# Reordering the first loads, casting and plain loads in a chain, and normalising two PSUM banks at once in a pooled-attention + MLP kernel

## Chip, cores, metric

One core of a Trainium2 chip. The metric is the time of one execution in device microseconds. All runs compared below are of the fast state; a ratio is the mean time of one kernel's fast runs over the mean of the other's fast runs of the same rounds, so it is not quite the ratio of the medians that are quoted.

## The reference

Attention whose keys and values are averaged over groups of 8 positions, followed by an MLP on every token.

```python
# q, k, v: (8, 8, 576, 64) float32: batch, head, position, dimension
k_p = k.reshape(B, H, 72, 8, D).mean(axis=3)      # 72 pooled keys per head
v_p = v.reshape(B, H, 72, 8, D).mean(axis=3)
attn = softmax(q @ k_p.T / sqrt(D))
x = (attn @ v_p).transpose(0, 2, 1, 3).reshape(4608, 512)
h = x @ w_in                                       # (512, 2048)
out = (h - tanh(h)) @ w_out                        # (2048, 512)
```

## The kernel before

In the lines of the profile PE is TensorE, the matrix engine, DVE is VectorE, ACT is ScalarE, POOL is GpSimd, and SP only issues transfers. PSUM, which PE writes to, is used as eight banks (the changed kernel's tile `PS` is 128 x 8 x 512 in fp32). A casting load turns fp32 into bf16 on the way (the page lists 512 KB for a quarter of w1, which is 1 MB in fp32); w1 and w2 come as four such loads each, w2(0) being the first quarter of w2. Filler (`warm_pe`) is matmuls whose result nobody uses.

Tokens are worked in nine groups of 512 (one batch is 576 tokens). A group has a hidden phase (16 tiles of 4 matmuls with w1, each followed by tanh and a subtraction) and an o phase (64 matmuls with w2). Attention of the next batch is woven into the o phase of the present group. Group 0 can't start until batch 0's attention has gone through by itself. Keys come as 8 heads x 72 pooled rows: 128 rows of each pair of heads go into "pairs" 0 to 3, and the 16 rows left over of each of the four pairs share a fifth tile ("leftover"), with index `NM` = 4.

```python
    load_main(k_pairs, k_raw[0], 0, 0, 1)               # SP: pair 0
    load_q0(0, 2)                                       # ScalarE's queue: heads 0, 1
    load_main(k_pairs, k_raw[0], 0, 1, 2)               # SP: pair 1
    load_q0(2, 4)
    load_main(k_pairs, k_raw[0], 0, 2, 4)               # SP: pairs 2, 3 (512 KB)
    load_q0(4, 8)                                       # heads 4 to 7 (512 KB)
    load_dense(k_pairs, k_raw[0], 0, nc.scalar)         # leftover keys (128 KB)
    load_dense(v_pairs, v_raw[1], 0, nc.scalar)         # leftover V (128 KB)
    ...
    nc.gpsimd.memset(q_bf[64:128, R, :, :], 0.0)
    ...                                                 # masks
    nc.gpsimd.dma_start(out=v_bf[:, 0:NM, :], in_=v_pairs[0, 0:128, :, :])   # V, cast to bf16
    ...
    for c in range(4):
        load_w1(c)                                      # casting loads, GpSimd's queue
    load_w2(0)
    load_w2(1)
    ...
    after(load_k(1), w1_dmas[1])                        # batch 1's keys wait for w1's 2nd quarter
    load_q(1, False)
    load_main(v_pairs, v_raw[1], 1, 0, NM)              # v1, behind q on SP
    ...
    pool_k(0, nc.vector, 2, 4)
    warm_pe(6)                                          # filler matmuls
    k_turn(2, 4)
    pool_k(0, nc.vector, NM, NT)
    ...
    av_half(0, 0, 0, xs[0], ps_all)                     # eight of these: AV of one half block,
    ...                                                 # 1 reciprocal, 1 product each
```

The softmax here doesn't subtract the row's maximum and nothing guards it: scores larger than these inputs give would overflow.

## Time and profile before

| | before |
|---|---|
| time, median of 3 | 300.87 us (300.75 to 301.25) |
| span, TensorE clock | 299.1 us, 1.000 |
| PE starts batch 0's AV (attention times V) | 14.61 us |
| five half hidden tiles done, PE dense | 21.27 us |
| o phase of group 0 starts | 34.55 us |
| group 1 starts | 54.98 us |
| from group 1's start to the end | 244.1 us |

The last five rows are read from the timeline of PE, by the first matmul of each kind. The prediction shows the other lines of this profile. One more view: the DMA issues of the first 5 us. Its columns are the number of transfers, KB of each, and microseconds from issue to landing.

```profile
k_raw<-in_k_dram SPq DMA_DIRECT2D x1, 512.0 KB, 6.1
q_raw<-in_q_dram ACTq DMA_DIRECT2D x1, 512.0 KB, 7.1
v_raw<-in_v_dram POOLq DMA_DIRECT2D x1, 512.0 KB, 8.6
k_raw<-in_k_dram ACTq DMA_DIRECT2D x1, 128.0 KB, 7.3
```

Pairs 2, 3 land at 7.83; the second half of q at 8.96, the leftover keys at 9.66. VectorE pools them in that order.

### The profile page before, as it was taken

How to read it: one execution, taken by the hardware profiler on the slowest of the kernel's cores; microseconds unless marked ns; L12 is line 12 of the kernel's file. 1: busy time of each engine (PE TensorE's matmuls, PEld its weight loads, DVE VectorE, ACT ScalarE, POOL GpSimd, SP SyncE). 2: the span in 40 equal slices, each digit the busy share in tenths (PEclk: the TensorE clock that was granted, in tenths of full speed). 3: DMA queues.
4: the chain of work that ended last, by engine and by line, in shares of the span. 5: the costliest groups of instructions: out<-in, count | busy, mean ns of one | idle time of the engine just before them, and what ended most of it. 6: DMA issues, size and time to landing. Idle time of an engine off the chain costs nothing.

```text
span 299.1 us, 4694 instructions
## 1 busy us (share of the span) xinstructions
PE 291.5 (97%) x1671; PEld 142.5 (48%) x1671; DVE 159.1 (53%) x343; ACT 149.4 (50%) x283; POOL 115.5 (39%) x110
## 2 busy tenths in 40 slices
PE   7989999999999999999999999999999999999994
PEld 3454455544544454445444554455445544444443
DVE  5658665673547444753476247716680758108600
ACT  4647583666146633654265516650665166126511
POOL 8500904871496109922971089307940000000000
PEclk9999999999999999999999999999999999999999
DMA  7999999849854998699648974897431430111032
GB/s 251 226 211 278 311 227 310 263 87 328 234 113 99 271 297 134 117 302 245 107 88 235 300 167 94 242 294 159 97 66 35 95 92 0 37 70 36 0 72 70
DMA packets 66183, 49.79 MB, mean 166 GB/s; under 512 B 39920, under 2 KB 52976, under 8 KB 66160
## 3 DMA queue, kind: packets, MB, share of 16 engines
q1 hardware_dynamic: 58832, 42.94, 56.0%
q0 software_dynamic: 4752, 4.72, 9.4%
q10 hardware_dynamic: 2576, 1.84, 2.3%
q8 instruction: 13, 0.21, 0.3%
q14 instruction: 10, 0.08, 0.1%
HBM read 36.70 MB, written 9.44 MB: 154 GB/s over the span
## 4 chain that ended last, share of the span: by engine, by line
PE 85%; DMA 9%; POOL 4%; issue 0%; SPq 0%; ACT 0%; DVE 0%; POOLq 0%
PE o_ps L456 40%; PE hT_ps L428 37%; DMA w1b<-in_moe_w_in_dram 4%; PE x_ps L346 4%; DMA k_raw<-in_k_dram 4%; PE s_ps L298 3%; POOL k_raw L198 1%; DMA out_dram<-o_sb 1%; POOL k_raw L203 1%; POOL kd L206 1%; POOL w2b L510 0%; PE xT_ps L390 0%; POOL v_raw L576 0%; PE qT_ps L171 0%; POOL w1b L503 0%
## 5 line engine op out<-in xcount | busy, mean ns | idle before, releaser
L456 PE MATMUL o_ps<-w2b,gT 128*128 128x512 bf16 x560 | 134.4, 380 | 0.0
L441 DVE TENSOR_TENSOR gT<-hT_ps,t_sb 128x512 bf16<-128x512 f32 x144 | 98.9, 691 | 57.7 <-ACT t_sb L439 57.6
L428 PE MATMUL hT_ps<-xT,w1b 128*128 128x512 bf16 x576 | 126.9, 379 | 0.3 <-ACT xT L397 0.3
L439 ACT ACTIVATE t_sb<-hT_ps 128x512 f32<-128x512 f32 x144 | 85.6, 597 | 38.3 <-PE hT_ps L428 37.5
L428 PEld LDWEIGHTS <-w1b 128*128 128x128 bf16 x576 | 55.9, 98 | 66.5 <-issue 0.4
L456 PEld LDWEIGHTS <-gT 128*128 128x128 bf16 x560 | 52.5, 98 | 52.0 <-issue 1.4
L465 ACT COPY o_sb<-o_ps 128x512 f32<-128x512 f32 x33 | 19.3, 585 | 75.2 <-PE o_ps L456 75.2
L359 DVE RECIPROCAL rden<-x_ps 128x4 f32<-128x4 f32 x80 | 14.2, 177 | 52.5 <-PE x_ps L346 52.0
L360 DVE TENSOR_TENSOR x_sb<-x_ps,rden 128x256 bf16<-128x256 f32 x80 | 34.0, 425 | 3.5 <-DMA xT<-x_sb 0.6
L148 POOL CAST q_bf<-q_raw 128x2048 bf16<-128x2048 f32 x6 | 11.3, 1888 | 59.9 <-issue 34.8
L198 POOL TENSOR_TENSOR k_raw<-k_raw 128x1280 f32<-128x1280 f32 x7 | 20.2, 2886 | 27.4 <-DMA k_raw<-in_k_dram 16.6
L317 ACT ACTIVATE E<-s_ps 128x288 bf16<-128x288 f32 x60 | 21.4, 410 | 13.2 <-PE s_ps L298 13.0
L346 PE MATMUL x_ps<-VB,E 128*128 128x130 bf16 x240 | 20.8, 221 | 0.4 <-ACT xT L397 0.3
L346 PEld LDWEIGHTS <-E 128*128 128x128 bf16 x240 | 16.9, 98 | 8.8 <-DVE VB L230 0.6
L216 POOL TENSOR_TENSOR v_raw<-v_raw 128x1280 f32<-128x1280 f32 x6 | 17.4, 2898 | 0.0
L298 PE MATMUL s_ps<-qT,KB 128*128 128x288 bf16 (+5 forms) x128 | 17.0, 290 | 0.2
L298 PEld LDWEIGHTS <-KB 128*128 128x128 bf16 (+1 forms) x128 | 7.0, 96 | 10.2 <-issue 3.5
L527 PE MATMUL warm_ps<-xT 128*128 128x512 bf16 x29 | 10.2, 465 | 1.3 <-DVE xT L539 1.3
L206 POOL TENSOR_TENSOR kd<-k_raw 128x640 bf16<-128x640 f32 x7 | 10.8, 1540 | 0.5
L203 POOL TENSOR_TENSOR k_raw<-k_raw 128x640 f32<-128x640 f32 x7 | 10.8, 1541 | 0.5
L397 ACT CAST xT<-xT_ps 128x256 bf16<-128x256 f32 (+1 forms) x14 | 5.8, 436 | 8.5 <-PE xT_ps L390 5.1
L219 POOL TENSOR_TENSOR v_raw<-v_raw 128x640 f32<-128x640 f32 x6 | 9.3, 1544 | 0.5
(73 smaller groups left out, 100.7 us busy)
## 6 DMA issues: line engine op xcount, KB each, us to landing
k_raw<-in_k_dram SPq DMA_DIRECT2D x7, 1024.0 KB, 5.9
q_raw<-in_q_dram SPq DMA_DIRECT2D x7, 1024.0 KB, 10.2
v_raw<-in_v_dram SPq DMA_DIRECT2D x7, 1024.0 KB, 9.3
out_dram<-o_sb SPq DMA_DIRECT2D x38, 128.0 KB, 2.4
out_dram<-o_sb SPq DMA_DIRECT2D x16, 256.0 KB, 3.7
w1b<-in_moe_w_in_dram POOLq DMA_DIRECT2D x4, 512.0 KB, 14.2
w2b<-in_moe_w_out_dram POOLq DMA_DIRECT2D x4, 512.0 KB, 16.9
k_raw<-in_k_dram SPq DMA_DIRECT2D x7, 128.0 KB, 5.8
```

Source lines behind the costliest of these rows:

```text
L198: first = eng.tensor_tensor(out=r[:, :, 0:4, :], in0=r[:, :, 0:4, :], in1=r[:, :, 4:8, :], op=ALU.add)
L216: eng.tensor_tensor(out=r[:, :, 0:4, :], in0=r[:, :, 0:4, :], in1=r[:, :, 4:8, :], op=ALU.add)
L298: nc.tensor.matmul(dst[p : p + w], lhsT=KB[b % 2][:, o : o + w], rhs=qTs[b][:, m, c0:c1], start=True, stop=True,)
L317: nc.scalar.activation(out=E[:, t, half * hs : (half + 1) * hs], in_=ps[:, :], func=ACT.Exp, scale=SCALE)
L346: nc.tensor.matmul(ps[:, 2 * n : 2 * n + 2, :].rearrange("p h d -> p (h d)") if n < 2 else ps.rearrange("p (a s) d -> p a s d", s=2)[:, :, ...
L359: nc.vector.reciprocal(out=rden[:, :, :], in_=ps[:, :, D:D1])
L360: nc.vector.tensor_tensor(out=x_sb[:, half, :, :], in0=ps[:, :, 0:D], in1=rden[:, :, :].to_broadcast([128, 4, D]), op=ALU.mult,)
L428: nc.tensor.matmul(h_tiles[i][:, :], lhsT=w1b[:, fb, i * 128 : (i + 1) * 128], rhs=xT[:, fb, tok0 : tok0 + TG], start=(fb == 0), stop=(fb ...
L439: nc.scalar.activation(out=t_sb[:, :], in_=h_ps[:, :], func=ACT.Tanh)
L441: nc.vector.tensor_sub(out=gT[:, :], in0=h_ps[:, :], in1=t_sb[:, :])
L456: nc.tensor.matmul(o_ps[:, :], lhsT=gts[i][:, tb * 128 : (tb + 1) * 128], rhs=w2b[:, i, :], start=(i == 0), stop=(i == NHID - 1),)
L465: (nc.vector.tensor_copy if g == 0 and tb % 2 else nc.scalar.copy)(out=o_sb[:, :], in_=o_ps[:, :])
```

## The change

The intent: (1) leftover keys go ahead of pairs 2, 3 on SP, so that the small tile is out of the way early; (2) PSUM becomes one tile with hand-chosen banks, and the AV of two blocks in two adjoining banks is normalised by one reciprocal and one product; (3) casting loads (w1, w2) and plain loads (batch 1's k, q, v) no longer run side by side but in a chain; (4) batch 1's q comes as nine consecutive rows per partition, without a tail in 256-byte pieces; (5) the last store falls on the last lane of the final waits.

```diff
+    nc.vector.memset(k_raw[0][:, NM, :], 0.0)
     nc.vector.memset(zeros, 0.0)
-    nc.vector.memset(k_raw[0][:, NM, :], 0.0)
...
+    load_dense(k_pairs, k_raw[0], 0)
+    load_q_main(0, 4, 8, nc.scalar)
     load_main(k_pairs, k_raw[0], 0, 2, 4)
-    load_q0(4, 8)
-    load_dense(k_pairs, k_raw[0], 0, nc.scalar)
     load_dense(v_pairs, v_raw[1], 0, nc.scalar)
...
-    nc.gpsimd.memset(q_bf[64:128, R, :, :], 0.0)
...
     nc.gpsimd.dma_start(out=v_bf[:, 0:NM, :], in_=v_pairs[0, 0:128, :, :])
+    nc.gpsimd.memset(q_bf[64:128, R, :, :], 0.0)
...
-    load_w2(0)
-    load_w2(1)
-    after(load_k(1), w1_dmas[1])
-    load_q(1, False)
-    load_main(v_pairs, v_raw[1], 1, 0, NM)
+    qt0 = load_q_tail(0)
+    k1 = load_k(1)
+    load_dense(v_pairs, v_raw[1], 1)
+    load_q_nine(1, 0, nc.sync)
+    load_q_nine(1, 1, nc.sync)
+    after([qt0], w1_dmas[1])
+    load_w2(0)
+    after(w2_dmas, qt0)
+    load_w2(1)
+    after([load_main(v_pairs, v_raw[1], 1, 0, NM)], w2_dmas[0])
...
+    pool_k(0, nc.vector, NM, NT)
+    warm_pe(2)
     pool_k(0, nc.vector, 2, 4)
-    warm_pe(6)
+    k_turn_left()
+    warm_pe(4)
     k_turn(2, 4)
-    pool_k(0, nc.vector, NM, NT)
...
+    def av_pair(p, half, b0):
+        ps = PS[:, b0 : b0 + 2, 0 : 4 * D1].rearrange("p k (h d) -> p k h d", d=D1)
+        for k in range(2):
+            av_mms(0, 2 * p + k, half, ps[:, k, :, :])
+        rden = work.tile([128, 2, 4, 1], FP32, name="rden2", tag="rden2")
+        nc.vector.reciprocal(out=rden[:, :, :, :], in_=ps[:, :, :, D:D1])
+        nc.vector.tensor_tensor(out=x0[:, 2 * p : 2 * p + 2, half, :, :], ...)
...
-    av_half(0, 0, 0, xs[0], ps_all)          # and seven more
+    av_pair(0, 0, 2)                         # and three more, with x0_turn between
```

(Not printed here: the helpers for the nine-row q, the leftover of batch 1's V turned by a matmul with `spread`, and the output rows of batch 1 in nines.)

## The prediction

> **What bounds the kernel now.** I read the page first, then PE's waits, the chain, the timeline of the first 56 us by engine, the DMA landings, and the last 5 us.
>
> ```profile
> PE   7989999999999999999999999999999999999994
> DMA  7999999849854998699648974897431430111032
> ```
>
> PE, the matrix engine, is full from the fourth slice (22 us) to the end, with one dip; the DMA engines are full up to about 44 us. From 55 us on, PE's work has no gap: in the chain 64 matmuls of 128x512 take 13.81 us, 0.216 us each, over and over. So only the first 55 us and the end can give anything.
>
> ```profile
> PE warm_ps L527 <- DVE xT L539: 1.3, 1, 1.3
> PE xT_ps L390 <- DVE x_sb L360: 0.7, 2, 0.4
> PE kT_ps L259 <- POOL kd L206: 0.5, 1, 0.5
> PE x_ps L346 <- ACT xT L397: 0.3, 1, 0.3
> ```
>
> These waits look small only because the program fills the start with warm_ps matmuls, which are no work. The figure to watch is when real MLP work becomes dense:
>
> ```profile
> 14.61 0.69 PE L346 MATMUL x_ps<-VB,E 128*128 128x130 bf16 x9
> 15.00 0.18 DVE L359 RECIPROCAL rden<-x_ps 128x4 f32<-128x4 f32 x1
> 15.22 0.42 DVE L360 TENSOR_TENSOR x_sb<-x_ps,rden 128x256 bf16<-128x256 f32 x1
> 19.63 0.43 DVE L360 TENSOR_TENSOR x_sb<-x_ps,rden 128x256 bf16<-128x256 f32 x1
> 20.41 5.78 PE L428 MATMUL hT_ps<-xT,w1b 128*128 128x512 bf16 x26
> ```
>
> (Start, duration.) Batch 0's attention starts AV at 14.61, VectorE normalises eight half blocks one after the other until 20.06, and PE is dense from 20.41. All five opened hidden tiles have their first halves at about 21.27 (20.41 plus four matmuls). The second place is batch 1's keys:
>
> ```profile
> 5.86 12.86 DMA w1b<-in_moe_w_in_dram
> 18.73 0.38 SPq L102
> 19.21 10.84 DMA k_raw<-in_k_dram
> 30.21 2.90 POOL k_raw L198
> 33.11 1.47 POOL w2b L510 x2
> 37.82 0.45 PE kT_ps L259 x5
> ```
>
> The key load waits for the second quarter of w1 (18.71), lands only at 30.05, GpSimd pools it until 37.77, and PE loses 0.52 us. Third, the DMA engines:
>
> ```profile
> 11.20:12.10 0.90, 0.79 (x4) 0.20 (x4) 0.60 (x2) 0.90 (x3) 0.90 (x3) 1.00 1.24 204
> 12.20:15.80 3.60, 3.12 (x35) 1.97 (x34) 2.10 (x8) 1.03 (x2) 1.43 (x3) 1.00 1.22 196
> ```
>
> Last column: GB/s, a casting load counted at its bf16 size. Alone (first row) casts write 204; with the 128 KB q tail mixed in (second row) all together write 196, and the packet counts of the trace give the cast only some 155 of 200 packets per us.
>
> [...]the two q tails (256 B pieces) take 8.1 and 9.0 us to land for 128 KB. [...]where keys of 2048 B run beside casts (25 to 28 us) the packet counts are 92 to 92 per us. [...]the trace's 128x512 subtraction has 691. [...]
>
> **The change part by part.**
>
> *Two-bank AV.* Eight times (0.18 + 0.42, which is 0.55 from start to start) becomes four times (0.18 + 0.69, by the overlap of the subtractions about 0.83): 4.4 becomes 3.3 us of VectorE, saving 1.1. The PSUM pool becomes one tile with hand-chosen banks; in steady state the same engines are waited for, so I count nothing there.
>
> *Leftover keys early.* They land near 6.1 instead of 9.66, as third transfer of SP. VectorE pools them (1.07 us) from 7.3 to 8.4, before pairs 2, 3, which then take 8.4 to 10.0 (before: 7.86 to 9.46). Then 0.23 for the leftover copy and 0.6 for the two key copies: 11.0. ScalarE's q copies end at 11.7, so the exponentials come at 11.7, 12.2 and 12.7, the last done at 13.3 (before 13.76). V follows at once: with two separate banks the first V half is placed by 14.0, the second by 14.45. AV may start at 14.05 and VectorE's first reciprocal at 14.5 instead of 15.0: 0.5 us.
>
> *PE after that.* VectorE's pairs end at about 15.4, 16.2, 17.1 and 17.9 (before 20.06: 2.1 us earlier). But PE must wait for the 0.6 us copies into xT: the first half tile opens at 17.15; then five half tiles (10 x 0.216) and 8 transposes (0.45) follow without a wait, so that all five are open at about 19.8. Against 21.27 that is **1.5 us**.
>
> *Loads.* Gone from 12 to 25 us: two 256 B q tails and four small V loads on ScalarE's queue; batch 1's q now comes in nine consecutive rows per partition (2304 B pieces, no tail). Estimates from the packet counts: a cast megabyte alone takes 2.6 us, so the casts end V at 11.1, w1 at 13.6, 16.2, 18.7, 21.3; with 0.45 to land, the second quarter is there at about 16.7 instead of 18.71. The order of waits of the changed kernel shows the next chain: q tail 0 waits for that quarter, the SP queue then carries k1, leftovers, q1, and both first w2 quarters wait for the tail. A transfer on another queue shows its first packet 3.4 us after issue under load (three cases: 3.3 to 3.6). So: tail issued until 17.4, packets from 20.8 to 22.4, landed 22.9; keys until 25.3, landed 25.8 with leftovers; w2(0) issued until 23.7, first packet 27.2, half shared with the end of q1, landed about **31.7**. PE wants it when the hidden phase ends, 34.55 - 1.5 = 33.05: no stall, 1.3 us of slack.
>
> *Key wait.* GpSimd starts at 25.8, needs 2.90 + 0.75 + 1.57 + 1.54 plus gaps: keys done at 32.6; PE asks at 34.8. The wait goes: **0.52 us**.
>
> *A new wait.* v1's main load now waits for w2(0): issued 31.8, first packet 35.5, shared with w2(2) and w2(3) at 0.17 us per pair of packets, landed about 41.4 (before 40.77). Then VectorE 1.49 + 0.82 + 0.2 + 0.43 + 0.65 and gaps: leftover sum at 44.0, VB at 45.2. PE asks for the sum at 43.8 and for VB at about 44.8 (before: x_ps at 47.05, minus 2.02, minus 0.25 for the tail scores that move behind it). I count **-0.6 us**.
>
> *Last lane.* SP at the end waits for the DMA semaphores one after the other, 62 ns each. The last store of before sits on the fourth of eight in order; four waits follow it. Now it is on the last two: **0.25 us**.
>
> Sum: 1.5 + 0.52 - 0.6 + 0.25 = 1.7 us, 300.87 - 1.7 = 299.2.
>
> **The rivals.** (1) w2(0) comes late and takes the place of the removed waits. For: it is issued 15 us later than before (8.05), behind a 256 B tail that took 8 to 9 us each time. Against: those two shared the engines with several queues. If the tail lands at 25 instead of 22.9, w2(0) lands near 34, PE stalls 1 us, v1 slips too and its stall becomes 2 to 3 us: 301 to 302. (2) V1 comes early enough, or the start is better than PE's copies suggest: the full 2.1 us of VectorE reach PE and no V wait: 300.87 - 2.1 - 0.52 - 0.25 = 298.0. (3) The start is hidden anyway, because w1's later quarters hold PE back. Against: they land at 19.2 and 21.8 by my count, wanted at 24 and 28; even before's 22.06 and 26.46 would do. It would leave 0.8 us: 300.1.
>
> **Range and chances.** The centre is 299.2. The start is uncertain by 0.6, the V wait by 0.8, w2(0) by 1 on one side: 297.8 to 300.8. A gain over 2% needs 6 us, more than all idle time of the first 55 us that the change touches; a loss over 2% needs a 6 us stall on w2. Faster 0.02, same 0.96, slower 0.02.
>
> **What would show it.** The last VectorE product of batch 0 at 17.9; the first MLP matmul near 17.2; q tail 0 landing near 23 and w2(0) near 31.7; no PE wait for kd; a PE wait of some tenths for vl or VB near 44; PE entering group 1 (the first 64-matmul block, before at 55.02) at about 53.6; one or no lane wait after the last store's landing. Wrong if PE waits for a w2 quarter, if V lands after 43, or if PE's waits appear after 55 us, where I expect none.

## The result, and the profile after

The changed kernel took 303.07 us (median of 4 runs, 302.12 to 303.33) against 300.81 us (4 runs, 300.46 to 301.25) of the kernel before in the same rounds: ratio 1.0069, 95% interval 1.0043 to 1.0094. It is within 2%, but slower, and outside the range. Timed again later over more rounds: 303.15 us, ratio 1.0074 (1.0053 to 1.0095).

Waits of PE in the changed kernel (total, number, longest), to be held against the four waits that the prediction shows:

```profile
PE PS L375 <- DVE kd L292: 3.1, 2, 1.9
PE PS L642 <- DVE xT L650: 1.8, 1, 1.8
PE PS L506 <- DVE x_sb L456: 0.3, 1, 0.3
PE PS L543 <- ACT xT L799: 0.2, 1, 0.2
```

The first is new. `kd` is batch 0's pooled keys, and the 3.1 us stand ahead of two transposes (PE's timeline; start, duration, and in brackets the idle time just before):

```profile
9.85 0.23 PE L375 MATMUL PS<-ident,kd 128*128 128x128 bf16 x1 [1.16 <-DVE kd L292]
12.90 0.29 PE L375 MATMUL PS<-ident,kd 128*128 128x128 bf16 x2 [1.95 <-DVE kd L292]
18.02 1.21 PE L470 MATMUL PS<-VB,E 128*128 128x130 bf16 x18
21.55 0.59 PE L543 MATMUL PS<-xT,w1b 128*128 128x512 bf16 x2 [0.24 <-ACT xT L799]
```

Before, the same two transposes of pairs 2, 3 ran at 9.52 and AV began at 14.61. VectorE's timeline says what it waited for, and the DMA issues of the first 5 us say how late that was:

```profile
8.72 0.43 DVE L284 TENSOR_TENSOR k_raw<-k_raw 128x256 f32<-128x256 f32 x1 [1.33 <-DMA k_raw<-in_k_dram]
11.23 0.69 DVE L284 TENSOR_TENSOR k_raw<-k_raw 128x512 f32<-128x512 f32 x1 [1.43 <-DMA k_raw<-in_k_dram]
```

```profile
q_raw<-in_q_dram ACTq DMA_DIRECT2D x1, 512.0 KB, 6.9
k_raw<-in_k_dram SPq DMA_DIRECT2D x1, 512.0 KB, 8.8
v_raw<-in_v_dram POOLq DMA_DIRECT2D x1, 512.0 KB, 9.9
k_raw<-in_k_dram SPq DMA_DIRECT2D x1, 128.0 KB, 7.0
```

Pairs 2, 3 are now issued at 2.44 (before at 1.72), since SP needs 0.68 us to issue the leftover load, and take 8.8 instead of 6.1 us: they land at 11.21 instead of 7.83. The leftover keys gained only 0.96 us (8.70 instead of 9.66).

Then a second thing shows, in the page's slices (PE's busy tenths and TensorE's granted clock, 40 slices):

```profile
PE   7599999999999999999999999999999999999995
PEclk9989999999999999999999999999999999999999
```

The third slice has a clock of 0.8. By windows (length; busy time of PE, PEld, DVE, ACT, POOL; then the clock, DMA share and GB/s):

```profile
6.97:10.38 3.41, 2.23 (x14) 0.86 (x12) 1.41 (x5) 2.77 (x6) 1.75 (x4) 1.00 1.11 259
10.38:13.79 3.41, 1.46 (x15) 0.79 (x13) 2.25 (x6) 0.35 (x1) 1.40 (x3) 1.00 1.24 208
13.79:17.21 3.42, 3.42 (x25) 1.63 (x24) 0.52 (x2) 2.37 (x5) 0.00 (x0) 0.50 1.24 205
```

PE was idle for more than half of 10.38 to 13.79, and for the 3.42 us that follow its clock is halved, just when it has to do scores and V. The two-bank step itself looks as predicted: 0.21 and 0.69 us, 0.85 from start to start.

```profile
18.65 0.21 DVE L778 RECIPROCAL rden<-PS 128x8 f32<-128x8 f32 x1 [0.23 <-PE PS L470]
18.89 0.69 DVE L779 TENSOR_TENSOR x<-PS,rden 128x512 bf16<-128x512 f32 x1
19.50 0.20 DVE L778 RECIPROCAL rden<-PS 128x8 f32<-128x8 f32 x1
```

The ledger from PE's timelines, in stages (us):

| stage | before | after | difference |
|---|---|---|---|
| AV starts | 14.61 | 18.02 | +3.41 |
| AV start to five half tiles done | 6.65 | 6.13 | -0.52 |
| to the start of the o phase | 13.28 | 13.39 | +0.11 |
| o phase of group 0, with batch 1's attention | 20.43 | 19.90 | -0.53 |
| group 1 to the end | 244.09 | 243.79 | -0.30 |
| span (rounded) | 299.1 | 301.2 | +2.1 |

So two gains are there (AV section, last lane) and one loss, larger than both, which the prediction had entered as a gain of 0.5. The o phase's 0.53 proves nothing yet: a late PE meets no key wait even with the old loads (19.73 in e2_only_keys below). That the key wait is really gone is shown by the runs whose start is mended.

### The profile page after: what moved, and what is told of

Same layout as the page of the kernel before. It is cut to its first block, busy times and chain, and to the rows that moved or that the text cites. A ratio compares the mean times of both kernels' runs of the same rounds, so it can differ in the third digit from the quotient of the medians.

```text
span 301.2 us, 4716 instructions
## 1 busy us (share of the span) xinstructions
PE 291.8 (97%) x1674; PEld 143.4 (48%) x1674; DVE 158.0 (52%) x336; ACT 148.7 (49%) x279; POOL 115.3 (38%) x110
## 4 chain that ended last, share of the span: by engine, by line
PE 90%; DMA 4%; DVE 3%; ACT 1%; issue 0%; SPq 0%; DVEq 0%
PE PS L571 40%; PE PS L543 39%; PE PS L470 4%; PE PS L414 4%; DMA k_raw<-in_k_dram 3%; DVE gT L556 1%; DMA out_dram<-o_sb 1%; PE PS L506 0%; PE PS L729 0%; ACT t_sb L554 0%; PE PS L642 0%; PE PS L791 0%; PE PS L247 0%; DVE x_sb L456 0%; DVE k_raw L284 0%
## 5 line engine op out<-in xcount | busy, mean ns | idle before, releaser
L571 PE MATMUL PS<-w2b,gT 128*128 128x512 bf16 x560 | 134.3, 379 | 0.0
L556 DVE TENSOR_TENSOR gT<-PS,t_sb 128x512 bf16<-128x512 f32 x144 | 98.9, 691 | 57.3 <-ACT t_sb L554 57.2
L543 PE MATMUL PS<-xT,w1b 128*128 128x512 bf16 x576 | 126.7, 379 | 0.3 <-ACT xT L799 0.2
L554 ACT ACTIVATE t_sb<-PS 128x512 f32<-128x512 f32 x144 | 85.6, 597 | 38.1 <-PE PS L543 37.7
L580 ACT COPY o_sb<-PS 128x512 f32<-128x512 f32 x33 | 19.3, 586 | 75.3 <-PE PS L571 75.3
L455 DVE RECIPROCAL rden<-PS 128x4 f32<-128x4 f32 x72 | 12.7, 177 | 51.0 <-PE PS L470 50.7
L456 DVE TENSOR_TENSOR x_sb<-PS,rden 128x256 bf16<-128x256 f32 x72 | 30.5, 424 | 2.5
L432 ACT ACTIVATE E<-PS 128x288 bf16<-128x288 f32 x60 | 21.4, 409 | 13.2 <-PE PS L414 13.0
L470 PEld LDWEIGHTS <-E 128*128 128x128 bf16 x240 | 16.7, 98 | 8.0 <-DVE VB L337 0.3
L470 PE MATMUL PS<-VB,E 128*128 128x130 bf16 x240 | 20.2, 220 | 0.2
L414 PE MATMUL PS<-qT,KB 128*128 128x288 bf16 (+5 forms) x128 | 17.5, 299 | 0.0
```

Of the source, the lines that this page charges most:

```text
L414: nc.tensor.matmul(dst[p : p + w], lhsT=KB[b % 2][:, o : o + w], rhs=qTs[b][:, m, c0:c1], start=True, stop=True,)
L432: nc.scalar.activation(out=E[:, t, c0:c1], in_=ps, func=ACT.Exp, scale=SCALE)
L455: nc.vector.reciprocal(out=rden[:, :, :], in_=ps[:, :, D:D1])
L456: nc.vector.tensor_tensor(out=x_sb[:, half, :, :], in0=ps[:, :, 0:D], in1=rden[:, :, :].to_broadcast([128, 4, D]), op=ALU.mult,)
L470: nc.tensor.matmul(ps[:, 2 * n : 2 * n + 2, :].rearrange("p h d -> p (h d)") if n < 2 else ps.rearrange("p (a s) d -> p a s d", s=2)[:, :, ...
L543: nc.tensor.matmul(h_tiles[i][:, :], lhsT=w1b[:, fb, i * 128 : (i + 1) * 128], rhs=xT[:, fb, tok0 : tok0 + TG], start=(fb == 0), stop=(fb ...
```

## The experiments

Twelve runs, all with correct output. The stages of each run's profile, in the columns of the ledger (us; V wait = PE's waits for the pooled V of batch 1):

| run | median us | ratio to before (95%) | AV starts | AV to open | o phase | V wait | group 1 starts | rest |
|---|---|---|---|---|---|---|---|---|
| before | 300.81 | 1 | 14.61 | 6.65 | 20.43 | 0 | 54.98 | 244.09 |
| after | 303.07 | 1.0069 (1.0043 to 1.0094) | 18.02 | 6.13 | 19.90 | 0 | 57.44 | 243.79 |
| e1_keys_back | 301.68 | 1.0013 (0.9984 to 1.0042) | 14.72 | 6.05 | 21.90 | 1.7 | 56.06 | 243.80 |
| e2_only_keys | 302.81 | 1.0048 (1.0016 to 1.0080) | 16.90 | 6.31 | 19.73 | 0 | 56.23 | 244.06 |
| e3_q_behind | 303.48 | 1.0071 (1.0029 to 1.0113) | 18.56 | 6.13 | 19.90 | 0 | 57.99 | 243.83 |
| e4_fill | 302.36 | 1.0032 (0.9997 to 1.0067) | 16.90 | 6.13 | 20.45 | 0.2 | 56.87 | 243.84 |
| e5_v_nine0 | 300.65 | 0.9986 (0.9971 to 1.0002) | 15.38 | 6.04 | 20.34 | 0 | 55.15 | 243.76 |
| e6_v_nine1 | 301.41 | 1.0014 (0.9996 to 1.0031) | 15.07 | 6.05 | 21.34 | 1.2 | 55.86 | 243.85 |
| e7_split_norm | 300.85 | 0.9992 (0.9977 to 1.0007) | 15.03 | 6.27 | 20.30 | 0 | 54.98 | 243.78 |
| e8_v_load_later | 300.30 | 0.9977 (0.9959 to 0.9996) | 14.66 | 6.05 | 20.55 | 0 | 54.66 | 243.80 |
| e9_tail_sooner | 299.83 | 0.9973 (0.9944 to 1.0002) | 14.52 | 6.05 | 20.01 | 0 | 53.97 | 243.81 |
| e12_best_again (as e9) | 299.83 | 0.9971 (0.9950 to 0.9993) | 14.55 | 6.05 | 20.09 | 0 | 54.08 | 243.81 |
| e10_after_v_later | 302.41 | 1.0045 (1.0023 to 1.0068) | 19.05 | 6.13 | 19.90 | 0 | 58.47 | 243.84 |
| e11_after_again | 303.15 | 1.0074 (1.0053 to 1.0095) | 19.03 | 6.13 | 19.90 | 0 | 58.46 | 243.85 |

Each profile is one execution, and the start of AV scatters with the first landings; the stage lengths after it repeat to 0.1 us.

### e1_keys_back: everything but the new key order

```diff
-    load_dense(k_pairs, k_raw[0], 0)
-    load_q_main(0, 4, 8, nc.scalar)
     load_main(k_pairs, k_raw[0], 0, 2, 4)
+    load_q_main(0, 4, 8, nc.scalar)
+    load_dense(k_pairs, k_raw[0], 0, nc.scalar)
...                       # and memsets, pooling, transposes, filler, scores in the order of before
```

> The changed kernel with only the order of batch 0's key transfers and their pooling put back (pairs 2, 3 third on SP, the leftover behind the second half of q on ScalarE's queue). Theory A (the leftover, issued ahead of pairs 2, 3, costs their place in the common order of transfers and delays the whole start): pairs 2, 3 land near 7.8 us instead of 11.2, AV starts near 14, no low clock near 14 us, and the time is 299.5 to 300.5 (the rest of the change gives its gain, less a wait of up to 1.5 us for w2(0) or batch 1's V, which land 9.3 us after q's tail). Theory B (the loads chained behind q's tail are what costs): the time stays at 302 to 303, with PE waiting for w2 or V.

Measured 301.68 us, ratio 1.0013: better than the changed kernel, but above the 299.5 to 300.5 expected. Pairs 2, 3 land at 7.92, AV starts at 14.72, the clock is 1.0 throughout. So the new key order was most of the loss. But the kernel still doesn't beat the one before, because a wait that the late start had hidden comes out. PE's longest wait, and its place in the timeline:

```profile
PE PS L332 <- DVE vl L322: 1.5, 1, 1.5
```

```profile
46.05 0.20 PE L332 MATMUL PS<-vl,spread 128*128 128x64 bf16 x1 [1.55 <-DVE vl L322]
47.56 0.39 PE L470 MATMUL PS<-VB,E 128*128 128x130 bf16 x4 [0.17 <-DVE VB L356]
```

`vl` and `VB` are batch 1's pooled V. Its load waits for the first quarter of w2 (landed 33.89) and lands at 43.28; before it landed at 40.77. The load chain keeps its own time: in the changed kernel w2(0) landed at 34.01 and V at 43.36, practically the same times, and only because PE was 3 us late there did nobody wait.

### e2_only_keys: nothing but the new key order

```diff
-    load_main(k_pairs, k_raw[0], 0, 2, 4)
+    load_dense(k_pairs, k_raw[0], 0)
     load_q0(4, 8)
-    load_dense(k_pairs, k_raw[0], 0, nc.scalar)
+    load_main(k_pairs, k_raw[0], 0, 2, 4)
...                       # in the kernel before; memsets, pooling, transposes, filler follow that order
```

> The kernel before with only the new order of batch 0's key transfers and pooling. Theory A: pairs 2, 3 land near 11 us, AV starts 3 us later than in the kernel before, the time is 303 to 304.5 (a loss of 2.5 to 3.5 us). Theory B: within 0.5 us of the kernel before.

Measured 302.81 us, ratio 1.0048, a loss of 2.0 us in the medians where 2.5 to 3.5 was expected. Pairs 2, 3 land at 11.10, AV starts 2.29 us later than before, and PE shows the same wait for `kd` (2.8 us) as the changed kernel. The new key order alone makes the old kernel slower. Its clock was full in the profiled execution (two successive stretches, same columns as above, counted from where its clock became full, 7.80):

```profile
7.80:11.21 3.41, 2.21 (x10) 0.66 (x8) 1.09 (x4) 2.36 (x5) 2.00 (x4) 1.00 1.15 254
11.21:14.63 3.42, 1.70 (x14) 0.91 (x14) 2.27 (x6) 1.29 (x3) 2.18 (x4) 1.00 1.22 199
```

It took 302.0 us. The other three took 302.6 to 303.0 with a mean clock of 0.993 to 0.994: it was a near thing. The changed kernel's first four runs part in the same way: 302.12 at 0.999, 302.96 to 303.33 at 0.993 to 0.994.

### e3_q_behind: leftover first, pairs 2, 3 ahead of q's second half

```diff
     load_dense(k_pairs, k_raw[0], 0)
-    load_q_main(0, 4, 8, nc.scalar)
     load_main(k_pairs, k_raw[0], 0, 2, 4)
+    load_q_main(0, 4, 8, nc.sync)
```

> The changed kernel, leftover still ahead of pairs 2, 3, but the second half of batch 0's q is issued on SP behind them instead of on ScalarE's queue beside them. Theory A in its sharper form (transfers of both queues land in the order in which they were issued, so pairs 2, 3 fell behind that megabyte-half of q): pairs 2, 3 land near 8.5 us and q near 10, the time falls to 299.5 to 301. If it is the leftover transfer itself that is slow (64 partitions, or the wait for its memset), pairs 2, 3 still land after 10 us and the time stays above 302.

Measured 303.48 us, where 299.5 to 301 was expected: a miss. The landings moved as expected for the keys, not for q: leftover keys at 6.79, pairs 2, 3 at 8.83, but q's second half only at 12.91 (issued at 3.06, 9.9 us). The wait changed its name:

```profile
k_raw<-in_k_dram SPq DMA_DIRECT2D x1, 512.0 KB, 6.4
q_raw<-in_q_dram SPq DMA_DIRECT2D x1, 512.0 KB, 9.9
```

```profile
PE PS L201 <- ACT q_bf L184: 2.6, 1, 2.6
```

So the leftover load is not slow by itself, which was the other reading: with q's second half behind them, pairs 2, 3 land at 8.83 instead of 11.21, so that q is 2.4 of the 3.4 us by which they were late. Here too the clock was halved, from 13.61 to 17.02, so not all of AV's delay (18.56) is q's landing.

All the profiles of the new key order fit one reading. The 1.25 MB of pairs 2, 3, q's second half and the two leftovers compete though two queues issue them: the DMA engines are full (DMA share 1.11 from 6.97 to 10.38 us in the changed kernel), from 5 to 7 us SP's queue moves 0.14 MB and ScalarE's 0.54 there, against 0.50 and 0.26 in the kernel before, and the large one that is issued last, with a leftover in front, lands at about 11 to 13 us (11.10 in e2_only_keys, 12.91 here). An earlier issue does not always land much earlier: in e11_after_again q's half, issued at 1.83, landed at 11.10 and pairs 2, 3, issued at 2.44, at 11.15. The leftover keys land at 6.79 here and at 8.70 in the changed kernel, where ScalarE issues q's half 0.11 us after them; the prediction had 6.1. Before, the order was pairs, q, leftover: what PE wants first landed first (7.83, 8.96, 9.66).

### e4_fill: the changed kernel with 14 more filler matmuls

```diff
     pool_k(0, nc.vector, NM, NT)
-    warm_pe(2)
+    warm_pe(7)
     pool_k(0, nc.vector, 2, 4)
     k_turn_left()
-    warm_pe(4)
+    warm_pe(13)
     k_turn(2, 4)
```

> The changed kernel with 14 more filler matmuls in PE's two waits for pooled keys (8.7 to 9.9 and 10.9 to 12.9 us). Theory C (those waits let the clock fall to half for 3.4 us at 13.8, which costs about 0.9 us on top of the late keys): no low clock, mean clock above 0.998 in every run, and the time is 302.0 to 302.4. If the clock costs nothing on this path: 303.0 as the changed kernel.

Measured 302.36 us, with full clock in all four runs (0.999 to 1.0). PE's timeline, and the window of 3.41 us that was starved in the changed kernel:

```profile
12.93 0.28 PE L375 MATMUL PS<-ident,kd 128*128 128x128 bf16 x2 [0.21 <-DVE kd L292]
16.90 1.21 PE L470 MATMUL PS<-VB,E 128*128 128x130 bf16 x18
```

```profile
10.38:13.79 3.41, 3.20 (x23) 1.60 (x21) 2.50 (x6) 0.93 (x3) 2.49 (x4) 1.00 1.24 207
```

The keys are turned at the same time as without filler (12.93 and 12.90), but AV starts at 16.90 instead of 18.02, which is 3.97 instead of 5.12 us after them. So the halved clock is worth 1.1 us at AV. By group 1 half of it is lost again (56.87 against 57.44, 0.57 left), as V now comes a little late for the earlier PE: 0.55 more in the o phase. In time the two kernels differ by 0.7 us, with overlapping intervals; the trace is the better witness. They were run at other times. Of the 3.41 us at AV, then, 2.3 are the keys (e2_only_keys and e4_fill agree) and 1.1 the clock.

### e5_v_nine0 and e6_v_nine1: batch 1's V released sooner

```diff
-    after([load_main(v_pairs, v_raw[1], 1, 0, NM)], w2_dmas[0])
+    after([load_main(v_pairs, v_raw[1], 1, 0, NM)], nine0)    # e6: nine1
```

Both stand on e1_keys_back; `nine0` and `nine1` are the two halves of batch 1's q.

> The version with the key loads of batch 0 put back, and batch 1's V released when the first half of batch 1's q has landed (29.9 there) instead of the first quarter of w2 (33.9). Theory (two losses: late pairs 2 and 3, and a late V): V lands near 39 to 40 instead of 43.3, the wait for vl and VB is gone, w2(0) lands 0.3 to 1 later (34.2 to 34.9, wanted at 34.17), group 1 starts at 54.1 to 54.9, time 299.7 to 300.5. Rival (the loss of 0.8 of that version lies in the dearer PE and VectorE steps of the q-in-nines and spread path, not in V's lateness): PE's work between the o phase and group 1 stays near 21.9, group 1 starts near 56, time 301.5.

> The same, but V released when the second half of batch 1's q has landed (32.5). Theory: V lands near 41.5 to 42, a wait of 0.2 to 0.6 for vl is left, w2(0) lands as before that (33.9) without a stall, group 1 starts at 54.3 to 54.8, time 299.8 to 300.3. Rival: as for the other, near 301.5.

e5: 300.65 us, ratio 0.9986, a little above the 299.7 to 300.5 expected. V lands at 40.78, the V wait is gone, and the o phase takes 20.34 instead of 21.90. The rival (dearer PE and VectorE steps) is out but for some 0.2 us: without a wait of note in the o phase, the new steps take 19.90 (changed kernel) and the old ones 19.73 (e2_only_keys). A small new wait of 0.28 us, at 39.47, is for w2's second quarter, which now lands at 39.43 instead of 36.40.

e6: 301.41 us, a miss. Released 1.5 us sooner than in e1_keys_back (32.4 instead of 33.9), V landed only 0.2 sooner (43.09), and PE still waited 1.2 us. V was issued at 32.42, behind w2's third quarter (30.67); in e5 it was issued at 30.09, ahead of that quarter (31.27). This fits the landings, but no run moved that quarter alone.

### e7_split_norm: the two-bank step by itself

```diff
-        nc.vector.reciprocal(out=rden[:, :, :, :], in_=ps[:, :, :, D:D1])
-        nc.vector.tensor_tensor(...)                 # both banks
+        for k in range(2):
+            nc.vector.reciprocal(out=rden[:, k, :, :], in_=ps[:, k, :, D:D1])
+            nc.vector.tensor_tensor(...)             # bank k alone
```

It stands on e5_v_nine0; PE's program is the same.

> The version with V after the first half of q, with the two-bank normalisation done again bank by bank (eight reciprocals and eight products instead of four pairs), PE's order untouched: it sizes the two-bank step alone. If the prediction's 1.1 us of VectorE reaches PE, the five half tiles are open about 1.1 later than in the unsplit version (20.8 becomes 21.9) and the time rises by 1.1; if PE's copies into xT hide most of it, 0.3 to 0.6 later. Time 300.2 to 301.5.

Measured 300.85 us against 300.65 in the same rounds. VectorE's timeline shows the half steps, 0.55 from start to start, eight of them:

```profile
15.40 0.18 DVE L780 RECIPROCAL rden<-PS 128x4 f32<-128x4 f32 x1
15.62 0.42 DVE L781 TENSOR_TENSOR x<-PS,rden 128x256 bf16<-128x256 f32 x1
15.96 0.17 DVE L780 RECIPROCAL rden<-PS 128x4 f32<-128x4 f32 x1
19.44 0.42 DVE L781 TENSOR_TENSOR x<-PS,rden 128x256 bf16<-128x256 f32 x1
```

VectorE ends 4.46 us after its first reciprocal, unsplit 3.44 (15.93 to 19.37): 1.0 us of VectorE saved, as predicted (1.1). But from AV's start to the five open tiles it is 6.27 against 6.04: only 0.23 us reach PE, which works its way through transposes, copies and filler meanwhile.

### e8_v_load_later and e10_after_v_later: GpSimd's V load issued at 3.68 again

```diff
+    nc.gpsimd.memset(q_bf[64:128, R, :, :], 0.0)
     nc.gpsimd.memset(mask[:, :, :], 1.0)
...
     nc.gpsimd.dma_start(out=v_bf[:, 0:NM, :], in_=v_pairs[0, 0:128, :, :])
-    nc.gpsimd.memset(q_bf[64:128, R, :, :], 0.0)
```

e8 on e5_v_nine0, e10 on the changed kernel. The change moved one memset behind the issue of batch 0's V, so that this megabyte of reads enters the race 0.68 us sooner.

> The version with the old key order and V after the first half of q, and in addition GpSimd's clearing of the upper half of the last q block put back ahead of its issue of batch 0's V load, so that this load is issued at 3.68 as in the kernel before, not at 3.00. Theory (the change's earlier V load takes turns from pairs 2, 3 and the second half of q): pairs 2, 3 land at 7.8 to 8.0 (8.77 without this), q's second half at 8.9 to 9.2 (9.75), AV starts at 14.3 to 14.7 (15.38). The gain in time is capped at about 0.6, since the first quarter of w2 lands near 34.0: 300.0 to 300.3. Rival (those landings scatter from run to run by themselves): pairs 2, 3 anywhere from 7.9 to 8.8, time 300.6.

> The changed kernel with nothing but that clearing put back ahead of the V load. If the earlier V load is part of its loss, pairs 2, 3 land at 10.3 to 10.7 instead of 11.2 and the time falls from 303.0 to 302.3 to 302.7. If not (only leftover keys and q stand ahead of pairs 2, 3), they land at 11.0 to 11.2 and the time stays at 302.8 to 303.2.

e8: 300.30 us, ratio 0.9977. q's second half lands at 8.89 (and 8.80 and 8.99 in the two runs of the next version, 8.96 before), against 9.51, 9.75, 9.70 and 9.96 in the four profiles with the old key order and the early V load: no overlap, so with the early V load q comes about 0.8 us later. For pairs 2, 3 the two groups touch (7.86 to 7.92 against 7.92 to 8.77), so there the effect is not shown. AV starts at 14.66. In the changed kernel the same edit gave 302.41 against 303.15 us, but with overlapping intervals, and the execution that was profiled was its slowest (304.02), with pairs 2, 3 at 12.14 where 10.3 to 10.7 was expected: its size there stays open.

### e9_tail_sooner, e11_after_again and e12_best_again: one more link, and the check

```diff
-    after([qt0], w1_dmas[1])
+    after([qt0], w1_dmas[0])
```

On e8_v_load_later.

> That version with batch 0's q tail released by the first quarter of w1 (landed about 15.2) instead of the second (17.8), so that the tail, batch 1's k, q, V and w2 all move up. Theory: tail lands near 21.5, w2(0) near 32, w2(1) near 37, V near 39, no PE wait for w2 or V; w1's third and fourth quarters land up to 1.5 later without a wait. Group 1 starts at 53.8 to 54.2, time 299.5 to 299.9. Rival (w1's later quarters are then delayed past their use, or nothing is gained as the DMA engines are full anyway): 300.3 to 301.

> The changed kernel as it is, timed in more rounds beside the best version, since the clearing put back ahead of the V load gave 302.4 against 303.1 in two different calls. If that earlier V load is part of the loss, 302.8 to 303.3 here; if the difference was the scatter of the start between calls, 302.2 to 302.7. Pairs 2, 3 land at 10.9 to 11.3 with V issued at 3.0.

> The version with all three corrections (old key order, V released by the first half of q and issued after the clearing, q tail released by the first quarter of w1) timed again: 299.5 to 300.1, faster than the kernel before by 0.8 to 1.2 and than the changed kernel by 2.5 to 3.3. Rival: its lead over the kernel before came from two or three lucky starts; then 300.4 to 300.9.

e9: 299.83 us. The time came as expected, the landings mostly did not: released 2.7 us sooner, the q tail landed 1.3 sooner (22.79), w2(0) not at all (33.80), w2(1) 0.7 (38.25), V 0.6 later (41.06). The engines are full (9 tenths or more in all 40 slices from 12 to 32 us), and here an earlier issue mostly waited longer. But w2(1) was the one PE waited for (0.49 us in e8), and that wait is gone: none of the waits left in PE's list (1.3 us before the first filler, four of 0.2 to 0.3) is for a w2 quarter or for V.

One of e9's six runs took 302.31 us with a mean clock of 0.993, as most runs of the changed kernel have; it counts in the interval. Timed again as e12: 299.83 us, ratio 0.9971 (0.9950 to 0.9993). In the same rounds the changed kernel (e11, pairs 2, 3 at 11.15) took 303.15, so by the means (299.86 and 303.12) the corrected version takes 0.989 of its time. It beats the kernel before by 0.3%, far within 2%.

## Why the prediction was wrong, step by step

- **Leftover keys early: the step that failed.** It said that the leftover keys "land near 6.1", that pairs 2, 3 are pooled from "8.4 to 10.0", and booked 0.5 us gained. It gave pairs 2, 3 no landing of their own. Measured: leftover 8.70, pairs 2, 3 landed at 11.21, PE waited 3.1 us for `kd`, AV 3.41 us later. The step took the place on SP's queue for the place in the race. SP's issue of the leftover load lasts 0.68 us, in which ScalarE issues half a megabyte of q; pairs 2, 3 then stand behind it. From 5 to 7 us SP's queue moves 0.14 MB beside 0.54 of ScalarE's (before 0.50 beside 0.26), so the queues take from each other. The prediction had counted this for the later stage, 92 packets per us of keys beside 92 of the casts, but made no such count at the start. From 6.97 to 10.38 us the engines moved 259 GB/s here and 282 in the kernel before: the new order brought no bandwidth. It chose who is last, and that was what PE needs next.
- **A wait turned into a half clock: not foreseen at all.** 1.1 of the 3.41 us (e4_fill). The kernel before is not free of it: one of the seven runs of the kernel before that were timed beside e1 to e4 also had a mean clock of 0.994 (302.51 us). In the changed kernel the clock was 0.50 for 3.42 us (13.79 to 17.21), and in its second profile (e11) for twice as long (6.83 us, 11.46 to 18.29).
- **Two-bank AV.** Predicted 1.1 us of VectorE, and with the copies in between 5.75 us from AV to five open tiles (14.05 to 19.8), that is 0.9 less than before. Measured 6.05, 0.6 less, of which the two-bank step is 0.23 (e7_split_norm). The rest may be PE's new order with two blocks in one copy; no run tested it. The mechanism was right, the term too large by 0.3.
- **Key wait of batch 1.** Predicted -0.52. In the changed kernel PE came too late to meet it with the old loads either, which is luck. With the start mended it is gone for the predicted reason: in e1_keys_back GpSimd has the keys ready at 35.10, before at 37.76, and PE asks at 36.76. They landed at 28.11 (predicted 25.8, before 30.05). The prediction's "PE asks at 34.8" is a slip: 37.30 less 1.5 is 35.8, still later than its 32.6.
- **New wait for V.** Predicted 0.6 with V landing at 41.4. In the changed kernel there was none, only because PE came 3 us late. With the start mended, V landed at 43.28 and the wait was 1.7. The term was mis-sized: each link was a little late (w1's second quarter 17.03 for 16.7, q tail 24.21 for 22.9, w2(0) 33.89 for 31.7).
- **Last lane.** Predicted 0.25. From group 1's start to the end, all twelve profiles with the changed end take 243.76 to 243.85, the two without it 244.09 and 244.06: 0.26. It lies where it was predicted: from the last store's landing to the end of the span it is 1.23 us before and 0.98 after.
- **The rivals.** Rival 1 (w2(0) late, 301 to 302) named the right landings, 34, and the slip of V, but PE never waited for w2(0). Its time was nearest to e1_keys_back, where V's wait of 1.7 us is somewhat less than the "2 to 3 us" that it gave. None of the rivals had the start become slower than before. Of its own signs of being wrong one came: V landed after 43, at 43.36, though PE did not wait for it.

The sum with the measured terms: AV start +3.4, AV section -0.5, +0.1 in the hidden phase, key wait -0.5, last lane -0.3: +2.2 us, against +2.26 in the medians.

## What to carry to other kernels

The DMA engines were full here (DMA share 1.15 from 5 to 45 us in the kernel before, 1.17 in the changed one), and a load moved forward pushed something else back, whichever queue each was on: the leftover keys pushed pairs 2, 3 from 7.83 to 11.10 us (e2_only_keys), and pairs 2, 3 ahead of q's second half pushed that from 8.7 to 12.91 us (changed kernel and e3_q_behind). So list the landings in the order in which the consumer needs them, and put nothing in front of the one needed next, not even a small load whose issue takes 0.7 us. A load chain that hangs on other landings kept its own time (batch 1's V at 43.36 us in the changed kernel, at 43.28 with the start mended), so a slow start hid its lateness; mend the start before judging the chain. And count what a wait does to TensorE's clock (1.1 of the 3.41 us here), not only its length.

## What the runs show of the clock and of the loads

- A gap of PE of 1.95 us, in a window of 3.41 us with PE busy for 1.46, was followed by half clock in the changed kernel; e4_fill, which filled it (3.20 busy), kept the full clock. Of the windows of this length at full clock in the first 30 us of the profiles, those followed by half clock had PE busy for 0.34 (e3), 1.42 (e11), 1.46 (changed kernel) and 1.54 us (e10), all others for 1.70 (e2) or more; but at the end of e1 a window with 1.50 kept the full clock, so no limit was shown.
- The time to issue was small beside the transfer (0.68 us to issue a 128 KB load on SP, 7.0 to land), but here it decided which queue's next load came first: it put pairs 2, 3 (issued at 2.44) behind half a megabyte of ScalarE's queue (issued at 1.83) and helped to delay their landing by 3.4 us.
- With the engines full (9 tenths or more from 12 to 32 us in e9_tail_sooner), an earlier issue brought less than it was moved by. A q tail released 2.7 us sooner landed 1.3 us sooner (e9_tail_sooner), and 1 MB of V released 1.5 us sooner landed 0.2 us sooner (e6_v_nine1); released 3.8 us sooner, ahead of w2's third quarter, it landed 2.5 us sooner (e5_v_nine0).
